# Fused linear attention and MLP on one core: unread matmuls added, and the kv products of two batches put into one group

## Chip, cores, metric

One core of a Trainium2 chip. The metric is the device time of one execution in microseconds, as the median of repeated runs.

## The reference

```python
def _attn_ref(q, k, v, g_norm):                 # 8 batches, 8 heads, 576 rows, 64 wide
    kv = np.einsum('bhsd,bhse->bhde', k, v)
    out = np.einsum('bhsd,bhde->bhse', q, kv)
    rms = np.sqrt(np.mean(out * out, axis=-1, keepdims=True) + 1e-06)
    return out / rms * g_norm

def _moe_ref(x, g_ln, w_ch1, w_ch2):            # x: 8 x 576 x 512, hidden 2048
    ...                                         # layer norm: xn
    return x + np.maximum(xn @ w_ch1, 0.0) @ w_ch2
```

## The kernel before

The program gives TensorE the first and second layers of the MLP of batch after batch (`mm1`, `mm2`). Between their chunks an agenda places the attention of later batches: `at(slot, ...)` runs its function ahead of chunk number `slot`, and there are 32 slots for each batch: batch b's first layer takes slots 32b to 32b+15, its second layer 32b+16 to 32b+31. A chunk of four matmuls of 128x512 takes 0.86 us in the trace. Of the 576 rows of a batch, 512 make four tiles; the other 64, with those of a second batch, make a remainder tile.

```python
    def fill(n, p1=None):                       # unread matmuls, of zeros
        ...
        for _ in range(n):
            nc.tensor.matmul(p1, lhsT=fill_sb[:, :128], rhs=fill_sb, start=True, stop=True)

    fill(18)                                    # then batch 0's kv, which needs k's cast and v
    kv_a.mms()
...
    def kv_of(*bs):                             # weights 128x64, those around it 128x128
        kv_ps = ps_m.tile([128, len(bs), HP, D], f32, tag="misc", name="kv_ps")
        ...                                     # 40 matmuls for each batch, then two casts on ScalarE
...
    def finish(b, ts, p2, ...):                 # VectorE evicts, SyncE issues two stores
        ...
        first.dma_start(dsts[0][:, c0:c1], o_sb[:64, c0:c1])
...
        # Tile.turn: x of a tile is transposed by a DMA that SyncE issues
        nc.sync.dma_start_transpose(dst, self.xc_t)
...
    at(68, lambda: load_batches((("k", 4), ("v", 4), ("q", 4)),
                                turned_q(3), blks[2][2][:1, nK - 1, 511:]))
    at(100, lambda: load_batches((("k", 5), ("v", 5), ("q", 5)), turned_q(4)))
    at(132, lambda: load_batches((("q", 6), ("k", 6), ("v", 6), ("k", 7), ("v", 7)),
                                 turned_q(5)))
    at(115, lambda: kv_of(5))
    for s, bs, rem, x_at, tn in ((56, (3,), 1, 64, 69), (85, (4,), 3, 88, 94),
                                 (152, (6, 7), 5, 154, 160)):
        at(s, lambda bs=bs: kv_of(*bs))
        plan_tile(s + .1, lambda rem=rem: rem_tile(rem), tn, False, x_at)
    for b, at_q, at_o, step in ((3, 56.05, 67, 4.3), (4, 86, 97, 4.75),
                                *((b, 32 * b - 43.3, 32 * b - 32, 5) for b in range(5, B))):
        at(at_q, lambda b=b: turn_q_dma(b))     # transpose of q, by SyncE too
        for j in range(J):
            o = at_o + step * j
            plan_tile(o, lambda b=b, j=j: main_tile(b, j), o + 6, False)   # transpose at o + 6
```

## Time and profile before

| | kernel before |
|---|---|
| median of 3 runs | 288.02 us (287.99 to 288.05) |
| the run whose profile was given | 290.37 us, span 288.5 us, mean granted clock 0.993 |
| TensorE busy in it | 280.6 us (97%) |
| VectorE, ScalarE busy | 150.4, 152.9 us |

The unread matmuls at the start keep the array busy; nobody uses their result. The span runs from the first to the last instruction; the time of a run is about 1.9 us more.

### The profile page before, as it was taken

How to read it: one execution, taken by the hardware profiler on the slowest of the kernel's cores; microseconds unless marked ns; L12 is line 12 of the kernel's file. 1: busy time of each engine (PE TensorE's matmuls, PEld its weight loads, DVE VectorE, ACT ScalarE, POOL GpSimd, SP SyncE). 2: the span in 40 equal slices, each digit the busy share in tenths (PEclk: the TensorE clock that was granted, in tenths of full speed). 3: DMA queues.
4: the chain of work that ended last, by engine and by line, in shares of the span. 5: the costliest groups of instructions: out<-in, count | busy, mean ns of one | idle time of the engine just before them, and what ended most of it. 6: DMA issues, size and time to landing. Idle time of an engine off the chain costs nothing.

```text
span 288.5 us, 5777 instructions
## 1 busy us (share of the span) xinstructions
PE 280.6 (97%) x2302; PEld 159.2 (55%) x2302; DVE 150.4 (52%) x335; ACT 152.9 (53%) x334; POOL 44.2 (15%) x74
## 2 busy tenths in 40 slices
PE   7699999999999999999999999999999999999995
PEld 3479855996569644445444544444444444444444
DVE  5566207946997884675366565762578200220022
ACT  3367754796649733882289248920894076016500
POOL 8432630023025004100620020000000000000000
PEclk9799999999999999999999999999999999999999
DMA  7999999949988989994999897038202610131033
GB/s 207 199 205 204 199 183 190 228 94 172 149 164 131 187 134 176 212 133 97 155 221 190 144 128 163 18 63 173 58 18 60 106 36 0 41 83 24 0 74 73
DMA packets 67442, 36.76 MB, mean 127 GB/s; under 512 B 35536, under 2 KB 62548, under 8 KB 67416
## 3 DMA queue, kind: packets, MB, share of 16 engines
q0 software_dynamic: 28736, 18.29, 44.4%
q1 hardware_dynamic: 38168, 17.39, 31.3%
q10 hardware_dynamic: 512, 0.72, 0.8%
q8 instruction: 18, 0.29, 0.4%
q14 instruction: 8, 0.07, 0.1%
HBM read 36.71 MB, written 9.44 MB: 160 GB/s over the span
## 4 chain that ended last, share of the span: by engine, by line
PE 94%; DMA 3%; ACT 1%; issue 0%; DVE 0%; POOLq 0%
PE p L489 43%; PE p L473 43%; DMA v_in<-in_v_dram 3%; PE o_ps L281 3%; PE kv_ps L254 2%; PE p L206 1%; PE tp L192 1%; ACT m L476 1%; PE og_ps L293 0%; ACT xT_blk L410 0%; PE odd L233 0%; PE tp L408 0%; ACT xT_blk L334 0%; DVE ss L358 0%; PE o_part L566 0%
## 5 line engine op out<-in xcount | busy, mean ns | idle before, releaser
L473 PE MATMUL p<-xT_blk,w_sb 128*128 128x128 bf16 (+2 forms) x1024 | 132.0, 286 | 0.6 <-ACT xT_blk L334 0.3
L489 PE MATMUL p<-w_sb,m 128*128 128x512 bf16 (+2 forms) x608 | 128.2, 368 | 0.0
L476 ACT ACTIVATE m<-p 128x512 bf16<-128x512 f32 x144 | 85.2, 595 | 46.8 <-PE p L473 44.5
L473 PEld LDWEIGHTS <-w_sb 128*128 128x128 bf16 x1024 | 78.6, 98 | 44.7 <-issue 1.3
L489 PEld LDWEIGHTS <-m 128*128 128x128 bf16 x608 | 57.3, 98 | 63.0
L494 DVE SCALAR_TENSOR_TENSOR o_sb<-p,rstd,x_blk 128x512 f32<-128x512 f32 (+2 forms) x38 | 27.2, 720 | 47.7 <-PE p L489 47.5
L287 ACT ACTIVATE sq<-o_ps 128x512 f32<-128x512 f32 x35 | 20.9, 596 | 27.0 <-PE o_ps L281 26.8
L400 ACT ACTIVATE dev<-x_blk,st_blk 128x512 f32<-128x512 f32 x36 | 25.7, 714 | 13.1 <-DVE st_blk L386 13.1
L358 DVE TENSOR_REDUCE ss<-sq 128x8 f32<-128x512 f32 x35 | 23.6, 678 | 16.4 <-ACT sq L287 16.4
L392 DVE SCALAR_TENSOR_TENSOR xc<-x_blk,st_blk,g_ln_sb 128x512 bf16<-128x512 f32 x34 | 25.6, 752 | 1.5 <-DVE st_blk L386 0.3
L363 DVE TENSOR_TENSOR y<-o_ps,inv 128x512 f32<-128x512 f32 x33 | 22.8, 692 | 3.1
L382 DVE SCALAR_TENSOR_TENSOR x_blk<-y,g_norm_sb 128x512 f32<-128x512 f32 x33 | 22.8, 692 | 1.1
L375 DVE RECIPROCAL inv<-rms 128x8 f32<-128x8 f32 x36 | 7.2, 201 | 22.9 <-ACT rms L368 22.9
L482 DVE RECIPROCAL rstd<-rstd 128x4 f32<-128x4 f32 x9 | 1.6, 174 | 30.8 <-ACT rstd L481 30.7
L368 ACT ACTIVATE rms<-ss,eps_sb 128x8 f32<-128x8 f32 x36 | 10.6, 295 | 11.6 <-DVE ss L358 11.5
L281 PEld LDWEIGHTS <-qt 128*128 128x128 bf16 (+1 forms) x156 | 10.6, 102 | 6.3 <-issue 0.7
L281 PE MATMUL o_ps<-kv_pack,qt 128*128 128x128 bf16 (+1 forms) x156 | 13.8, 221 | 0.0
L98 POOL COPY gate<-qt 1x1 bf16<-1x1 bf16 x5 | 0.9, 176 | 82.1 <-DMA qt<-q_p 82.1
L206 PE MATMUL p<-fill_sb 128*128 128x512 bf16 x24 | 8.2, 489 | 1.3 <-DVE eps_sb L142 1.3
L259 ACT CAST kv_pack<-kv_ps 64x256 bf16<-64x256 f32 x7 | 2.6, 365 | 11.4 <-PE kv_ps L254 11.4
L400 ACT ACTIVATION_READ_ACCUMULATOR dev<-x_blk,st_blk 128x1 f32 x36 | 6.8, 189 | 0.0
L254 PEld LDWEIGHTS <-k_in 128*64 128x64 bf16 x280 | 4.9, 113 | 2.2 <-issue 2.1
(94 smaller groups left out, 118.2 us busy)
## 6 DMA issues: line engine op xcount, KB each, us to landing
out_dram<-o_sb SPq DMA_DIRECT2D x66, 128.0 KB, 2.4
w_sb<-in_moe_w_ch_dram POOLq DMA_DIRECT2D x7, 512.0 KB, 13.9
q_in<-in_q_dram POOLq DMA_DIRECT2D x7, 320.0 KB, 9.7
k_in<-in_k_dram POOLq DMA_DIRECT2D x7, 320.0 KB, 8.6
v_in<-in_v_dram POOLq DMA_DIRECT2D x7, 320.0 KB, 10.3
q_in<-in_q_dram POOLq DMA_DIRECT2D x8, 256.0 KB, 10.7
k_in<-in_k_dram POOLq DMA_DIRECT2D x7, 256.0 KB, 9.2
v_in<-in_v_dram POOLq DMA_DIRECT2D x7, 256.0 KB, 12.5
```

Source lines behind the costliest of these rows:

```text
L206: nc.tensor.matmul(p1, lhsT=fill_sb[:, :128], rhs=fill_sb, start=True, stop=True)
L281: nc.tensor.matmul(flat[rows, hp * 128:(hp + 1) * 128], lhsT=lhsT_of(hp), rhs=kvp[:, hp, :], start=True, stop=True)
L287: nc.scalar.activation(self.sq_t, self.o_ps, func=AF.Square)
L358: nc.vector.tensor_reduce(self.ss, self.sq_t, axis=AX.X, op=ALU.add)
L363: nc.vector.tensor_mul(self.y_t, self.o_ps, self.inv().to_broadcast([128, H, D]))
L382: nc.vector.scalar_tensor_tensor(x_blk[:, ts].rearrange("p (h d) -> p h d", h=H), in0=self.y_t, scalar=1.0, in1=g_norm_sb.to_broadcast([12 ...
L392: nc.vector.scalar_tensor_tensor(self.xc_t, in0=x_blk[:, self.ts], scalar=st[:, 1, self.ts:self.ts + 1], in1=g_ln_sb, op0=ALU.add, op1=ALU ...
L400: nc.scalar.activation(dev, x_blk[:, ts], func=AF.Square, bias=st[:, 1, ts:ts + 1], accum_out=st[:, 2, ts:ts + 1])
L473: nc.tensor.matmul(p1[:, i, :], lhsT=w1_sb[:, kk, de * 128:(de + 1) * 128], rhs=blk[2][:, kk, sl], start=(kk == 0), stop=(kk == nK - 1))
L476: nc.scalar.activation(m1[:, de0:de0 + per, sl], p1, func=AF.Relu)
L489: nc.tensor.matmul(p2[:, c0:c1], lhsT=m1s[b][:, de, ts * 128:(ts + 1) * 128], rhs=w2_sb[:, de, c0:c1], start=(de == 0), stop=(de == nDe - 1))
L494: nc.vector.scalar_tensor_tensor(o_sb[:, c0:c1], in0=p2[:, c0:c1], scalar=rstds[b][:, ts:ts + 1], in1=blks[b][0][:, ts, c0:c1], op0=ALU.mu ...
```

## The change

Its intent: to hide the wait for v with unread matmuls up to batch 0's kv, and to save one entry into and one exit from a half-column group (matmuls with weights of 128x64 among those of 128x128; about 0.11 us each, worked out in the prediction from pieces of 0.75 and 1.39 us), by joining kv of 4 and 5. For that, k and v of 5 must come earlier, and the remainder tile 3 and batch 4's tiles move behind the group. The transpose of batch 4's q goes from slot 86 to 91, and the loads of k and v of 6 from slot 132 to 101.

```diff
-    def fill(n, p1=None):
+    def fill(n, p1=None, rhs=fill_sb):
...
-    fill(18)
+    fill(6, fill(15), k_p[:, 0, :512])
...
-    at(68, lambda: load_batches((("k", 4), ("v", 4), ("q", 4)),
+    at(68, lambda: load_batches((("k", 4), ("v", 4), ("q", 4), ("k", 5), ("v", 5)),
                                 turned_q(3), blks[2][2][:1, nK - 1, 511:]))
-    at(100, lambda: load_batches((("k", 5), ("v", 5), ("q", 5)), turned_q(4)))
-    at(132, lambda: load_batches((("q", 6), ("k", 6), ("v", 6), ("k", 7), ("v", 7)),
+    at(101, lambda: load_batches((("q", 5), ("k", 6), ("v", 6)), turned_q(4)))
+    at(132, lambda: load_batches((("q", 6), ("k", 7), ("v", 7)),
                                  turned_q(5)))
-    at(115, lambda: kv_of(5))
-    ... (85, (4,), 3, 88, 94),
+    ... (98, (4, 5), 3, 100, 106),
-    ... (4, 86, 97, 4.75),
+    ... (4, 91, 101.5, 4.5),
```

More of the change, by code (lines that the diff above doesn't have):

```diff
@@ L205, in fill @@
         for _ in range(n):
-            nc.tensor.matmul(p1, lhsT=fill_sb[:, :128], rhs=fill_sb, start=True, stop=True)
+            nc.tensor.matmul(p1, lhsT=fill_sb[:, :128], rhs=rhs, start=True, stop=True)
         return p1
@@ L689 @@
     at(47, lambda: load_batches((("k", 3), ("v", 3), ("q", 3)), turned_q(2)))
-    at(68, lambda: load_batches((("k", 4), ("v", 4), ("q", 4)),
+    at(68, lambda: load_batches((("k", 4), ("v", 4), ("q", 4), ("k", 5), ("v", 5)),
                                 turned_q(3), blks[2][2][:1, nK - 1, 511:]))
-    at(100, lambda: load_batches((("k", 5), ("v", 5), ("q", 5)), turned_q(4)))
-    at(132, lambda: load_batches((("q", 6), ("k", 6), ("v", 6), ("k", 7), ("v", 7)),
+    at(101, lambda: load_batches((("q", 5), ("k", 6), ("v", 6)), turned_q(4)))
+    at(132, lambda: load_batches((("q", 6), ("k", 7), ("v", 7)),
                                  turned_q(5)))
     at(164, lambda: load_batches((("q", 7),), turned_q(6)))
-    at(115, lambda: kv_of(5))
-    for s, bs, rem, x_at, tn in ((56, (3,), 1, 64, 69), (85, (4,), 3, 88, 94),
+    for s, bs, rem, x_at, tn in ((56, (3,), 1, 64, 69), (98, (4, 5), 3, 100, 106),
                                  (152, (6, 7), 5, 154, 160)):
@@ L703 @@
     plan_tile(210, lambda: rem_tile(7), 216, False)
-    for b, at_q, at_o, step in ((3, 56.05, 67, 4.3), (4, 86, 97, 4.75),
+    for b, at_q, at_o, step in ((3, 56.05, 67, 4.3), (4, 91, 101.5, 4.5),
                                 *((b, 32 * b - 43.3, 32 * b - 32, 5) for b in range(5, B))):
```

## The prediction

The sum has its terms, -0.2 us for (b) alone and about -1.2 with (a), but that the six matmuls would do away with the half-rate window was supposition. The fills themselves have a granted clock of 1.00 in the trace, also while they ran 0.43 us apart.

> **What bounds the kernel now.** I read the page first, for which engine has no room:
>
> ```profile
> span 288.5 us, 5777 instructions
> PE 280.6 (97%) x2302; PEld 159.2 (55%) x2302; DVE 150.4 (52%) x335; ACT 152.9 (53%) x334; POOL 44.2 (15%) x74
> PEclk9799999999999999999999999999999999999999
> ```
>
> TensorE (PE) is busy in 97% of the span and no other engine in more than 55%. The missing 288.5 - 280.6 = 7.9 us is at the two ends: 1.3 us before the first unread matmul, 2.6 us before batch 0's kv, a few tenths near 17 us, and about 3.4 us of last eviction and store. The third line has the granted clock, in tenths: only the second slice (7.2 to 14.4 us) is low. The waits of TensorE say the same, for the whole run:
>
> ```profile
> PE even L233 <- DMA v_in<-in_v_dram: 2.6, 1, 2.6
> PE p L206 <- DVE eps_sb L142: 1.3, 1, 1.3
> PE p L473 <- ACT xT_blk L334: 0.3, 1, 0.3
> ```
>
> So the time can fall in only two ways: less TensorE work [...] in the long dense stretch, or an earlier start of that stretch. The change tries one of each. For the start I read windows cut where the clock changes. The columns after the stretch are its length, then busy time and (instructions) of PE, PEld, DVE, ACT, POOL, then the granted clock, the DMA share and GB/s:
>
> ```profile
> 4.47:7.89 3.42, 2.46 (x12) 0.98 (x10) 1.25 (x6) 1.15 (x1) 3.16 (x6) 1.00 1.14 254
> 7.89:11.30 3.41, 1.79 (x87) 1.52 (x88) 1.22 (x5) 0.67 (x2) 1.49 (x3) 1.00 1.46 195
> 11.30:14.71 3.41, 3.41 (x45) 2.20 (x38) 2.52 (x9) 1.98 (x6) 1.66 (x3) 0.50 1.32 205
> ```
>
> In the stretch with PE busy 1.79 of 3.41 us (52%) the clock is still full, and the next stretch, of the same length, runs at half. The stretch before, at 72%, was followed by a full one. For the second part I read the chain that ended last (start us, length us, what):
>
> ```profile
> 102.04 0.75 PE kv_ps L254 x40
> 102.79 0.23 PE o_ps L281 x8
> 129.92 0.75 PE kv_ps L254 x40
> 130.67 11.33 PE p L489 x52
> 163.61 1.39 PE kv_ps L254 x80
> 165.00 0.23 PE o_ps L281 x8
> 165.22 7.01 PE p L489 x32
> ```
>
> One batch of kv costs 0.75 us, two together 1.39, not 1.50; and the stretch behind a kv is too long for its matmuls. An undisturbed stretch (64 matmuls of 128x512 in 13.81 us, at 186.94 in the same view) gives 0.2158 us each: 52 of them are 11.22, but 11.33 are shown; 32 are 6.91, but 7.01 are shown.
>
> [...] The kv matmuls (128x64 weights) and the remainder tile's (128x64) use half the columns, all around them use 128; the trace agrees with about 0.11 us on entry (0.75 = 0.64 + 0.11, since two batches take 1.39 = 2 x 0.64 + 0.11) and 0.10 to 0.11 on exit, and nothing between kv and remainder tile (0.23 us for eight). [...] the transposes of x took 2.4 us to land when no load ran and up to 7.9 us when loads did.
>
> **The change, part by part.**
> (a) The unread matmuls: 18 become 15, plus 6 that read the cast of k. The 15 start as before; the first seven run [...] about 0.43 us apart until 4.47 us, the other eight at 0.216, so they end near 6.2 us instead of 6.8. The cast of k (VectorE, 5.90 to 6.66) releases the six; 6 x 0.216 = 1.3, so they end near 8.05. Batch 0's kv starts when v has landed (9.47) in either kernel: three added matmuls cost nothing on the path, and the wait shrinks from 2.6 to about 1.4 us. The only possible gain is the clock after 11.30 us. [...] What that is worth I followed by hand: the first square comes 0.2 us sooner; the three unread matmuls at 13.3 (1.28 us at half clock, 0.65 at full) and the small groups around them stop holding back tile 1's product, its square and the diagonal that ScalarE makes behind it; the first matmul of the dense part goes from 17.09 to about 16.1 us, 1.0 us earlier. w1's first quarter lands at 14.2, so it does not take this back. But the last third of w2 lands at 31.82 + 14.3 = 46.1 us and is used at about 47.1: at most some 0.95 us survive.
> (b) kv of 5 joins kv of 4 and the remainder tile in one half-column group. Same matmuls, one entry and one exit less: 0.11 + 0.11 = 0.22 us off TensorE, on the path, since TensorE never waits there. Sure, if nothing new waits.
> (c) The group moves from the second-layer stage (ScalarE busy 5.0 of 14.9 us) into batch 3's first-layer stage (12.6 of 14.7). Four casts of 0.37 us and the remainder tile's square, root and variance (0.6 + 0.3 + 0.9) come in, one tile of batch 4 partly moves out. Placing the ReLUs in turn behind these, the longest delay of one is about 1.2 us; with three buffers for p TensorE would stall only beyond about 1.7. So nothing.
> (d) Loads: ten instead of six transfers from 90.1 us. The like ten at 139.4 had landed at 147.2 + 14.0 = 161.2, 21.8 us after the first; that gives 111.9, and the group at slot 98 starts near 113.3. Margin 1.4 us.
> (e) Batch 4's tiles go back 4 slots. The last transpose of x is now queued behind a store that needs slot 120's result: VectorE done about 137.1, store issues 1.2 us, transpose issued near 138.3, landing in 2.5 us (as the one at 136.9 did) near 140.8; its first reader comes near 141.8. Margin 1.0 us, where it was 2.6.
> Sum: (b) alone -0.2; with (a) about -1.2.
>
> **The rivals.**
> First, the clock falls all the same: [...] Then 288.02 - 0.22 = 287.8. For the other side speaks that the six seem placed by their author to end just before v comes. I give both about half.
> Second, a transfer [...]: v of batch 5 late for slot 98, or the last transpose late for slot 128. The in-order TensorE would stand still for it, some 0.3 to 1.5 us, 288.0 to 289.3. Against it, the margins of (d) and (e); for it, that both are short and rest on landings under other traffic. About 15%.
> Third, ScalarE as the bound in batch 3's first layer: its 12.6 us become about 14 of some 16.2 (the stage gains 1.6 us with the group), so it stays below TensorE. Under 5%, and worth at most 0.5 us.
>
> **Range and chances.** Two lumps of nearly equal weight, 287.8 (clock falls) and 286.9 (clock held, w2 limiting), with a thin tail upward: the middle is 287.4, and 286.7 to 288.1 holds both with their scatter (the three runs before lie within 0.06). Two per cent would be 5.8 us; no part can bring or cost that, except a failure I do not see.
>
> **What would show it.** Right in (b): a kv piece of 80 matmuls near 113 us of 1.39 us, none near 130, and three lines of waits for TensorE as now. In (a): the wait for v near 1.4 us, and the second slice's clock at 9 instead of 7, with the first dense matmul near 16.1; or 7 and 17.1, then the first rival holds. Wrong: a wait of TensorE for k, v or xT between 105 and 145 us, or for w2 near 46; or a clock that falls one window later[...].

## The result, and the profile after

The changed kernel takes 291.56 us (median of 4, 291.50 to 292.15), the kernel before beside it 288.03. The ratio is 1.0127 (95% interval 1.0112 to 1.0142); ratios here are the mean time of one kernel's runs over that of the other's of the same rounds, so not quite the ratio of the medians. Executions over 1.5% slower than the fastest of the same kernel are left out of the means. That is 3.5 us slower, outside the range that was predicted (286.7 to 288.1).

The page of the changed kernel, top lines:

```profile
span 290.3 us, 5754 instructions
PE 280.2 (97%) x2280; PEld 158.9 (55%) x2305; DVE 151.0 (52%) x335; ACT 152.3 (52%) x334; POOL 44.0 (15%) x74
PEclk9999999999999999999999999999999999999999
```

TensorE's work is the same and the clock is full, yet the span is longer. The waits of TensorE (who waited for whom, us in total, times, longest) say by what:

```profile
PE p L473 <- DMA xT_blk<-xc: 3.1, 2, 1.9
PE p L206 <- DVE eps_sb L142: 1.3, 1, 1.3
PE p L473 <- ACT xT_blk L334: 0.3, 1, 0.3
PE p L473 <- ACT m L476: 0.2, 1, 0.2
```

Two waits for a transposed x are new, and one for ScalarE; the wait for v is gone. TensorE in order of time (start us, busy us, line, output and inputs, count, idle before) places the first wait and the one for ScalarE:

```profile
111.69 1.89 PE L473 MATMUL p<-xT_blk,w_sb 128*128 128x512 bf16 x8 [1.94 <-DMA xT_blk<-xc]
113.51 1.46 PE L254 MATMUL kv_ps<-v_in,k_in 128*64 128x64 bf16 x80
...
122.50 1.02 PE L473 MATMUL p<-xT_blk,w_sb 128*128 128x512 bf16 x4
123.69 2.75 PE L473 MATMUL p<-xT_blk,w_sb 128*128 128x512 bf16 x11 [0.16 <-ACT m L476]
...
143.82 4.48 PE L473 MATMUL p<-xT_blk,w_sb 128*128 128x512 bf16 x19 [1.17 <-DMA xT_blk<-xc]
```

The idle time shown is too small by about 0.16 us for each wait, because the modelled end of a matmul lies behind the start that the next could have had (four show 1.02 us busy, and 4 x 0.2158 is 0.86). The four matmuls at 122.50 would have let the next start at 122.50 + 4 x 0.2158 = 123.36; it started at 123.69, a delay of 0.33. In the same way the waits for x delay TensorE by 2.10 and 1.34 us (142.26 + 0.22 for four small matmuls = 142.48 against 143.82). The sum is 2.10 + 1.34 + 0.33 - 0.22 (one entry and one exit less) = 3.55 us. A second count gives the same: from the product of batch 3's last tile to that of batch 5's second one TensorE takes 49.91 us before (first two lines) and 53.46 after (last two), 3.55 more.

```profile
96.47 0.39 PE L281 MATMUL o_ps<-kv_pack,qt 128*128 128x128 bf16 x4
146.38 0.39 PE L281 MATMUL o_ps<-kv_pack,qt 128*128 128x128 bf16 x4
94.68 0.39 PE L281 MATMUL o_ps<-kv_pack,qt 128*128 128x128 bf16 x4
148.14 0.39 PE L281 MATMUL o_ps<-kv_pack,qt 128*128 128x128 bf16 x4
```

The medians differ by 3.53. But the profiled run is the slowest of the four, 292.15, which is 4.1 us more than the kernel before; the other 0.6 is laid to the start, which is taken up below. So the three delays are most of the loss, and the experiments have to show what makes each of them.

And the start? All runs of the kernel before beside the experiments have a granted clock of 0.998 to 1.000; the eleven beside the last two came at 287.93 to 288.20 us. The half-rate window in the trace that I read (granted clock 0.50 from 11.30 to 14.71 us) is an exception, and so is its v, which landed at 9.47 us; in the thirteen other profiles it landed at 8.14 to 8.48. The rows of the window table that the prediction leads with do not describe the run that is timed.

### The profile page after: what moved, and what is told of

It is laid out like the page before. It is cut to its first block, busy times and chain, and to the rows that moved or that the text cites. A ratio compares the mean times of both kernels' runs of the same rounds, so it can differ in the third digit from the quotient of the medians.

```text
span 290.3 us, 5754 instructions
## 1 busy us (share of the span) xinstructions
PE 280.2 (97%) x2280; PEld 158.9 (55%) x2305; DVE 151.0 (52%) x335; ACT 152.3 (52%) x334; POOL 44.0 (15%) x74
## 4 chain that ended last, share of the span: by engine, by line
PE 85%; DVE 4%; DMA 4%; ACT 4%; issue 2%; SPq 1%; DVEq 0%
PE p L473 39%; PE p L489 37%; DMA xT_blk<-xc 4%; PE p L206 3%; PE o_ps L281 2%; PE kv_ps L254 2%; ACT m L476 1%; DVE x_blk L382 1%; DVE y L363 1%; DVE ss L358 1%; DVE xc L392 1%; ACT rms L368 0%; PE tp L192 0%; ACT dev L400 0%; SPq L510 0%
## 5 line engine op out<-in xcount | busy, mean ns | idle before, releaser
L489 PE MATMUL p<-w_sb,m 128*128 128x512 bf16 (+2 forms) x594 | 126.6, 368 | 0.8 <-issue 0.2
L206 PEld LDWEIGHTS <-fill_sb 128*128 128x128 bf16 x27 | 3.2, 124 | 5.9 <-issue 3.8
```

The lines of the kernel that those rows point to most:

```text
L206: nc.tensor.matmul(p1, lhsT=fill_sb[:, :128], rhs=rhs, start=True, stop=True)
L489: nc.tensor.matmul(p2[:, c0:c1], lhsT=m1s[b][:, de, ts * 128:(ts + 1) * 128], rhs=w2_sb[:, de, c0:c1], start=(de == 0), stop=(de == nDe - 1))
```

## The experiments

Theory A: the two added loads keep the last transpose of batch 3's x from landing (first wait), and SyncE's issue queue holds the last transpose of batch 4's x (second wait): it follows issues that run without a pause from 134.23 to 141.22 us. Rival B: the moved group itself costs the time, loads or no loads. Rival C: the start costs it. The first four kernels take the change apart.

**Fills only** (fills_only). The kernel before with only the `fill` lines of the diff.

> The kernel before with only the fills changed (15, then 6 that wait for the cast of k). Theory: the unprofiled runs of before already take 288.0 where the profiled one took 290.4, so most runs of before have no half-rate window near 12 us, and the fills gain little: 287.7 to 288.1, with a full clock in the profile. Rival (my prediction's lump, fills are worth 1 us): 287.0. Rival that the loss comes from the start: over 289.

288.03 (5 runs) against 288.00, ratio 1.0003 (0.9991 to 1.0016). Neither a gain of 1 us nor the loss. Rival C falls for the bulk of the loss; tenths of a us at the start come back further down.

**The kv part only** (kv_part_only). The changed kernel with `fill(18)`.

> The changed kernel with the old 18 fills. Theory: the whole loss is in the kv part: 291.2 to 291.8, TensorE waiting for xT twice, about 1.9 us near 111 and about 1.2 near 143. Rival: without the new fills the start moves and the waits shrink or go: below 290.

291.41 against 288.00. Waits of 1.72 us at 110.95 and 1.21 at 143.12, and the one of 0.16 for ScalarE: by the same sum, 1.88 + 1.37 + 0.32 - 0.22 = 3.35, measured 3.41. The loss is in the kv part.

**Early loads only** (early_loads_only). The kernel before with the loads of k and v of batch 5 at slot 68; nothing else is moved.

```diff
-    ... (("k", 4), ("v", 4), ("q", 4)),
+    ... (("k", 4), ("v", 4), ("q", 4), ("k", 5), ("v", 5)),
-    ... (("k", 5), ("v", 5), ("q", 5)), turned_q(4)))
+    ... (("q", 5),), turned_q(4)))
```

> The kernel before, but k and v of batch 5 loaded at slot 68 behind those of 4; no matmul is moved. Theory (the two added loads keep the last transpose of batch 3 from landing): TensorE waits for xT where batch 3's first layer begins, 1.5 to 2 us, and perhaps again for the q of batch 4 whose transpose queues behind; 289.5 to 292. Rival (the moved group and tiles cost the time, not the loads): 288.0.

290.45 (290.27 to 292.47). The loads alone cost 2.4 us or more. The profile is of the slowest run, 292.47: in it the granted clock fell during the wait for q (1.00 from 112.80 to 113.20 us, a mean of 0.74 from 113.20 to 113.60), and the four matmuls at 114.11 took 0.61 us, where 0.39 is usual. The other three, with a clock of 1.000, came at 290.27 to 290.47. The waits of TensorE in the profile:

```profile
PE o_ps L281 <- DMA qt<-q_p: 2.3, 1, 2.3
PE even L233 <- DMA v_in<-in_v_dram: 1.5, 1, 1.5
...
PE p L473 <- DMA xT_blk<-xc: 0.4, 1, 0.4
```

The wait for x is smaller here than in the changed kernel: 0.4 and not 1.9. The group of kv 4 and the remainder tile (0.75 + 0.23 + 0.11 = 1.09 us) still stands in the stage ahead, so the reader of the transpose comes 1.09 us later. The q of batch 4, whose transpose stands behind that of x on SyncE, then comes late as well. SyncE in order of time shows it in the changed kernel (the issue of q's transpose, 3 us long in the kernel before, is held for 7.87):

```profile
103.19 1.30 SPq L412 DMA_TRANSPOSE xT_blk<-xc  x1
104.59 0.67 SPq L509 DMA_DIRECT2D out_dram<-o_sb  x1
105.31 0.60 SPq L510 DMA_DIRECT2D out_dram<-o_sb  x1
106.02 7.87 SPq L213 DMA_TRANSPOSE qt<-q_p  x1
```

**kv apart.** The changed kernel with the loads of 5 as before, kv of 4 alone at slot 98 with the remainder tile, kv of 5 at slot 115. Batch 4's tiles stay late.

> The changed kernel, but k and v of batch 5 loaded as before, kv of 4 alone at slot 98 and of 5 at slot 115; batch 4's tiles stay late. Theory: the first wait goes (1.9 us), the second, of the last transpose of batch 4 behind a store and the transpose of q, stays at about 1.2: 289.0 to 289.6. Rival (loads cause both): 288.0. Rival (the moved group itself costs): above 290.

289.20 (288.78 to 289.65). In its profile no wait near 111, one of 0.67 near 141 (a delay of 0.83). The first wait goes with the loads, the second stays with the late tiles, smaller than expected. The time is in the expected range all the same, by luck: of the 1.5 us that the profiled run (289.52) is slower, 0.83 are this delay, and about 0.5 lie at the start (first dense matmul at 15.39 us), which is explained further down.

**Batch 3's last transpose ahead of two stores.**

```diff
-            plan_tile(o, lambda b=b, j=j: main_tile(b, j), o + 6, False)
+            plan_tile(o, lambda b=b, j=j: main_tile(b, j), o + (3.9 if (b, j) == (3, J - 1) else 6), False)
```

> The changed kernel with the last transpose of batch 3's x issued ahead of the two stores that it stood behind (slot 83.8, not 85.9). Theory (it lands about 8 us after its issue while the five loads run, so an issue 2 us sooner is a landing nearly 2 us sooner): the wait of 1.9 near 111 falls to 0.3 or less, the one near 143 stays: 289.6 to 290.1. Rival (it lands when the loads are through, whenever it was issued): the wait stays and the time too, 291.4.

290.50 (290.31 to 290.85). The wait for x falls from 1.94 to 0.27, as theory A has it; but the expected 289.6 to 290.1 is missed, because a wait of 0.82 us for v of batch 5 appears inside the group, which the later x had hidden:

```profile
PE p L473 <- DMA xT_blk<-xc: 1.4, 2, 1.2
PE p L206 <- DVE eps_sb L142: 1.3, 1, 1.3
PE kv_ps L254 <- DMA v_in<-in_v_dram: 0.8, 1, 0.8
```

Slot 98 is itself too early for the loads: the last of the ten landed 18.3 us after its issue, where I had taken 14.0 from another place in the trace of before.

**Batch 4's last transpose ahead of two stores** (x4_ahead). The same edit with `4 if (b, j) == (4, J - 1)`.

> The changed kernel with the last transpose of batch 4's x issued ahead of the two stores of mm2's second tile (slot 119, not 121). Theory (the in-order issue queue, not the transfer, makes it late): issued 1.2 us sooner, landing in 2.5 as before, the wait of 1.2 near 143 becomes 0 to 0.2: 290.2 to 290.5. Rival (transfer under load): unchanged at 291.4.

Four runs: 290.35 and 290.40, and 292.30 and 292.73. The first two are in the expected range, with a clock of 0.998 to 1.000. The other two have 0.994 and 0.992, and the profile is of one of them: the wait near 143 is gone, but the one near 111 was 2.71 us, and a window with a granted clock of 0.51 followed (columns as in the prediction):

```profile
108.54:111.95 3.41, 0.70 (x5) 0.14 (x3) 0.75 (x1) 0.00 (x0) 0.00 (x0) 1.00 1.29 193
111.90:115.40 3.50, 3.46 (x8) 1.05 (x8) 0.00 (x0) 0.60 (x1) 0.63 (x2) 0.51 1.13 247
```

The long wait cost itself, and then came slow matmuls: the eight behind it took 3.56 us, and 1.89 in the changed kernel. So the median of 291.35 says little; the two runs at full clock support the theory, two runs only.

**Both ahead** (both_ahead).

> Both transposes ahead. Theory: only the delays on ScalarE behind the casts and the saved 0.2 us are left: 288.0 to 288.7. If the group moved into the first-layer stage costs TensorE nothing: 287.8. If over 289, a third loss is there that I have not named.

289.27 (288.66 to 290.10): above the expected 288.0 to 288.7. Its profile (289.21) has 0.27 for x, 0.16 for ScalarE, and a group of 80 that shows 1.77 us busy where 1.46 is its length in the same view of the changed kernel: a third loss of about 0.3, put down to v of batch 5 as above. A few tenths more lie at the start (first dense matmul at 15.04 us).

**The price of one group.** The kernel before with kv of 6 at slot 148, apart from that of 7.

```diff
+    at(148, lambda: kv_of(6))
-                                 (152, (6, 7), 5, 154, 160)):
+                                 (152, (7,), 5, 154, 160)):
```

> The kernel before with kv of 6 at slot 148 and of 7 at slot 152, instead of both at 152: the price of one more half-column group alone. Theory: one entry and one exit, 0.11 + 0.11 us: 288.22 against 288.00, and a piece of 40 matmuls of 0.75 us. Rival (drains are no cost on the path): 288.0.

"Drains" is the expectations' name, here and below, for the 0.11 us at the entry and at the exit; what happens in the array there is not shown.

288.37 against 288.04, 0.3 us slower by the medians and 0.2 by the ratio (1.0006); its interval (0.9994 to 1.0019) holds 1, because three of the eleven runs beside it came at 288.55 to 288.82. The profile has the two pieces, of 0.77 and 0.75 us. By the times alone it is not settled; the traces settle it. Between the tile products on both sides of the group TensorE takes 16.61 us before (155.46 to 172.07) and 16.84 here (153.32 to 170.16): 0.23 more for one entry and one exit.

**Group one slot later.** Both transposes ahead, batch 3's tiles in steps of 4.0 for 4.3, the group at slot 99, batch 4's tiles from 102 in steps of 4.3: the attempt to keep the gain.

> A try at keeping the gain: both transposes ahead, batch 3's tiles 0.3 slots closer so that the last transpose goes out sooner still, kv of 4 and 5 one slot later (99) so that v of 5 has landed, batch 4's tiles from 102 in steps of 4.3. Theory: the waits of 0.27 (xT) and 0.4 (v) of both_ahead go, 0.16 for ScalarE stays, the drains save 0.22: 287.9 to 288.2, no better than before beyond noise. Rival: something else moves late, over 288.6.

289.37: a miss. The group is back at 1.46 us, but 0.23 for x, 0.16 for ScalarE and a gap of about 0.3 us near 141 stay, and the dense part began at 15.17 us.

**No loads of 5** (no_loads_of_5; wrong result: relative error 0.48). The changed kernel with batch 4's last transpose ahead, and k and v of 5 not loaded; every matmul is where the changed kernel has it.

> Wrong result on purpose: the changed kernel with batch 4's last transpose ahead and k and v of batch 5 not loaded at all (kv of 5 works on what batch 3 left there). Every matmul and its place is as in the changed kernel. Theory: without the two loads no wait for xT near 111 and none for v; 0.16 for ScalarE stays, drains save 0.22: 287.9 to 288.1. Rival (the group's move brings the reader too near the transpose, load or no load): a wait of 0.5 or more near 111, over 288.4.

288.64 (288.15 to 288.80). No wait for x or v is left in its profile: rival B falls for the large part, the loads make the first wait. But 0.5 us over the expectation is unexplained by waits. Its first dense matmul started at 15.35 us, where profiles with the old 18 fills, other than that of the kernel before itself, have 14.75 to 14.95. TensorE at the start of the changed kernel shows the same:

```profile
1.34 6.29 PE L206 MATMUL p<-fill_sb 128*128 128x512 bf16 x15 [1.34 <-DVE eps_sb L142]
7.47 1.46 PE L206 MATMUL p<-k_in,fill_sb 128*128 128x512 bf16 x6
```

v landed 6.9 us after its issue at 1.25, so at 8.2 us. The six end at 7.47 + 1.46 = 8.93 (less the 0.16 above), and batch 0's kv waits for them: it starts at 8.86.

**No loads of 5, old fills** (wrong again).

> Wrong result on purpose: as no_loads_of_5, with the old 18 fills. Theory (the new fills end at 8.7 to 9.0 us in many profiles, behind v which lands at about 8.2, and so hold batch 0's kv back by up to 0.8 us): about 0.4 less than no_loads_of_5, 288.0 to 288.3, the first dense matmul near 14.8 and not 15.35. Rival (the fills are free, the 0.6 over before is in the kv part): 288.6 again.

288.22 (288.02 to 289.20) against 288.07, ratio 1.0010 (0.9998 to 1.0022); first dense matmul at 14.75. So the new fills cost about 0.4 us in this pair by the medians, and 0.6 by the starts in the two profiles; by the ratios it is 0.2, and their intervals overlap. And even without any load in the way the joined group is not faster: it saves 0.22 at entry and exit and loses 0.32 to ScalarE (chunk at 119.87 of four matmuls, the next at 121.05 and not 120.73).

**More fills.** The kernel before with `fill(24)`.

> The kernel before with 24 plain fills for 18. Theory: they outlast v in most runs (end between 8.0 and 9.7 us [...]), kv starts late: 288.4 to 289.2 with a wide spread. Rival (fills beside the wait for v are free): 288.0 as before. Rival of the prediction ([...] gains 1 us): 287.0.

288.48 (288.05 to 289.26) against 288.07, ratio 1.0020 (1.0008 to 1.0032): slower and wide, as fills that sometimes outlast v would be. No run shows a gain from a kept clock.

None of the twelve beats the kernel before.

## Why the prediction was wrong, by its own steps

**The baseline.** The prediction reads 17.09 us as the start of the dense part and hangs half of its weight on a half-rate window. Of the fourteen profiles only that one has it. In the four others with the old fills the start is at 14.75 to 14.95 and no such window is there (mean granted clock 0.998 to 1.000; 0.994 in early_loads_only, with its fall near 113 us): v lands at 8.3 to 8.5 us, not 9.5, and the wait ahead of kv is 0.3 to 1.5 us. No run came near the lump at 286.9; the fastest of all is 287.88. The hint was in hand: 290.37 for the profiled run beside 288.02.

**Step (a)** said that three added matmuls "cost nothing on the path". That holds where the fills become faster early. Their pace went from about 0.43 us for one to 0.22 at 4.5 us in the trace before and at 7.2 us in that of the changed kernel, with a granted clock of 1.00 on both sides. With a late change nearly all of the 15 fills run at 0.43 us (6.29 us for the 15 in the changed kernel), and the six end after v. The profiles with the new fills show it: where the 15 took 5.28 to 5.76 us (three of them) the dense part starts at 14.61 to 14.78, where they took 6.03 to 6.38 (five) at 15.04 to 15.39. Cost in the medians: 0.4 us between no_loads_of_5 and its twin with old fills, none seen in fills_only, 0.15 between the changed kernel and kv_part_only. Whether the new fills make the rare half-rate window rarer, no run here can say.

**Step (b)**, 0.22 us saved by one entry and one exit less, stands as a measured saving; what in the array takes the time is not shown. The chain of waits of the changed kernel has the joined group at the length that two batches took before at 163.61:

```profile
113.58 1.40 PE kv_ps L254 x80
...
165.38 1.39 PE kv_ps L254 x80
```

As a time of whole runs it is at the edge of what they resolve, but the traces have it: 0.23 us for one group more, and 0.22 less in the sum of 3.55.

**Step (c)** ended in "So nothing". It is 0.32 us: one ReLU is late enough to stop TensorE for want of a buffer for p. I had placed the ReLUs by hand behind ScalarE's own work, found 1.2 us as the longest delay, and held 1.7 to be harmless. What I left out is VectorE. In the changed kernel ScalarE stands idle for 1.20 us up to 121.67, because a root waits for VectorE's sum (`ss`); the ReLUs behind it go late, and the chunk that TensorE had ended at 121.40 is read from 123.06 on, 1.66 us later. In kv_apart, with two casts in the group for four, ScalarE is idle for 0.74 us at the same place and TensorE has no such wait. This delay alone eats the gain of (b). The third rival, given under 5%, came true in part: ScalarE did stop TensorE, by less than 0.5, but as a late ReLU and not as the bound of the stage.

**Step (d)** failed for the main part of the loss. It asked only whether the added loads would be in time for their own reader. It did not ask what else is in transfer in these 20 us, though the prediction itself has the 7.9 us of a transpose under load. The last transpose of batch 3's x was issued at 103.19 and landed 8.37 us later, at 111.56; in the kernel before it was issued at 105.62, landed in 2.5, and its reader came at 112.5. Besides, taking the group out of the stage ahead brought that reader 1.09 us sooner. early_loads_only (2.4 us slower, nothing moved) and no_loads_of_5 (wait gone, everything moved) show both sides of it. And the margin of 1.4 us for v of batch 5 itself was used up: the last load landed 25.3 us after the issue of the first (88.33 to 113.67), where (d) had 21.8, and waits of 0.3 to 0.8 came to light when the first one was taken away.

**Step (e)** had the right mechanism and the wrong length. It put the issue of batch 4's last transpose 3.5 us ahead of its reader; it was 1.3 us ahead of where the reader would have been (141.22 against 142.48). SyncE of the changed kernel shows the queue:

```profile
134.23 0.47 SPq L509 DMA_DIRECT2D out_dram<-o_sb  x1
134.75 0.59 SPq L510 DMA_DIRECT2D out_dram<-o_sb  x1
135.39 1.28 SPq L412 DMA_TRANSPOSE xT_blk<-xc  x1
136.78 3.10 SPq L213 DMA_TRANSPOSE qt<-q_p  x1
139.98 0.54 SPq L509 DMA_DIRECT2D out_dram<-o_sb  x1
140.57 0.59 SPq L510 DMA_DIRECT2D out_dram<-o_sb  x1
141.22 1.29 SPq L412 DMA_TRANSPOSE xT_blk<-xc  x1
```

From 134.23 on it issues without a pause, 7.0 us of it ahead of the transpose. I counted VectorE's end (137.1) and one pair of stores (1.2 us), and left out that the third tile's transpose (slot 116.5) had also moved behind the first stores and in front of q's: 1.4 us more ahead of q's 3.2, and the stores of VectorE's result wait for both. The landing was 2.47, as said.

**The second rival** ("v of batch 5 late for slot 98, or the last transpose late for slot 128", about 15%, up to 289.3) is what happened, twice over in one run, and beyond the size given.

## What to carry to other kernels

When loads are moved earlier, list every transfer that is issued while they run and find the slack of each one's reader; the moved load's own reader is only one of them. When work leaves the stage ahead of a reader, that reader comes sooner by the length of the work. Before building on a feature of a trace, compare the profiled run's own time with the timed runs: a feature worth 1 us in a run that is 2.4 us slow may belong to that run alone.

## What the traces show of transfers under load

- How long a small transpose waits beside queued loads: 8.4 us for the one issued at 103.19 among the ten transfers of five loads (the changed kernel), 3.5 us for the same one without the loads of k and v of 5 (no_loads_of_5), 2.5 for the last one of batch 4's x, at 141.22.
- How long the issue of a transpose itself is held: q's took 7.87 us on SyncE in the changed kernel, against 3.0 in the kernel before and 3.2 in no_loads_of_5, and the stores behind it waited too. It goes with the loads and not with the late transpose of x ahead of it: in x3_ahead, both_ahead and later_group x was in use by 109.4 to 109.9 us, and q's issue still ran to 112.6 or 112.7. It ended near the landing of the last load: at 113.89 and 113.67 us in the changed kernel, at 112.74 and 112.7 in x3_ahead.
